# Block attention with a gated MLP: from heads with split operands to pairs of heads in plain float32

## The chip, the cores and the metric

The kernel runs on one core of one Trainium2 chip. The metric is the device time in microseconds. Two runs of the kernel before took 1095.97 and 1096.88 us, median 1096.43 us.

## The reference

Attention over 8 batches of 8 heads, 576 positions, head size 64, with a mask by blocks of 64 positions. A gated MLP follows, and all of it is in float32:

```python
scores = (1/sqrt(64)) * q @ k.T              # per batch and head: 576 x 576
scores = where(i // 64 >= j // 64, scores, -1e9)
attn = exp(scores - max(scores)); attn = attn / (sum(attn) + 1e-9)
x = attn @ v                                 # heads side by side: 576 x 512 per batch
h = gelu_tanh(x @ w_in)                      # 576 x 1024
u, v = h[:, :512], h[:, 512:]
v_n = (v - mean(v)) / sqrt(var(v) + 1e-6) * g_ln
v_s = w_sg @ v_n + b_sg                      # mixes the 576 positions
out = x + (u * v_s) @ w_out
```

q and k come transposed (64 x 576 per head), v as 576 x 512 per batch; w_in, w_sg and w_out arrive in float64 or float32 and are split once into a high and a low part.

## The kernel before

Five engines work from queues of their own: PE (matrix products and transposes into PSUM banks of 512 columns), DVE and ACT (elementwise, both read PSUM), POOL (elementwise in SBUF), and SP, which issues every DMA. Each queue is worked off in order. The order within each queue is set by a scheduler when the program is built, from the order of the code and estimated times, so the code says what depends on what, and the built program what stands behind what.

**Products in two precisions.** `F32R` operands go through PE in one pass per column. To keep the precision, a float32 operand is cast to F32R (the high part) and the rest is kept as a second F32R operand (the low part). Plain `F32` operands need no split.

**Scores** (`load_qk`, `split_qk`, `Scores`, line 419). A head has only 64 rows of q and k. `load_qk` loads each head's q and k twice, into both halves of the 128 partitions (line 156). `split_qk` makes `q_s` (upper half the high part of q, lower half its rest: cast on DVE at line 94, subtraction on POOL at line 221), `k_h` (cast on ACT, line 94) and `k_l` (subtraction on POOL, line 222). One product with all 128 rows then gives high and low of q at once, and two products, with k_h and k_l, give the scores. The raw tiles `q_f` and `k_f` have one buffer each. The 576 query positions are cut into five row tiles i = 0 to 4 of 64, 128, 128, 128 and 128 rows, and tile i needs only its first 64, 192, 320, 448 or 576 key columns: 1600 columns per head, in four banks.

**Softmax.** `maximum` (DVE, line 432) masks, scales and takes the row maximum of a bank into the tile `prob`, `exponent` (ACT, line 446) exponentiates in place and sums.

**Values** (`Values`). `turn0`, `turn2` and `turn1` transpose `prob` on PE into a bank `ptj` (line 472), `high` casts it to `pt_h` (ACT, line 483), `low` makes `pt_l` (DVE, line 491), and `av0`, `av2`, `av1` multiply (line 538). `v_s` holds the high and the low part of v side by side in 128 columns, and so the result `ob` has the two parts in its two halves, which `fold` adds (a copy on ACT, an addition on DVE). `inverse`, `turn_sums` and `rows` spread the reciprocal row sums over a tile `rb`, and `normalise` multiplies on POOL, spills the result x to DRAM for the residual, and splits it for the MLP. The transposed banks come from a pool `p` of three, all others from a pool `s` of five.

`FAP` and `FSP` make exceptions for early pairs of heads: the first eight pairs (batches 0 and 1) take their products with the values in plain float32 ("w", line 518), pairs 0 and 3 their scores too, and pair 1 splits its scores in three products ("p").

**The MLP** is cut in pieces: `v_part` (5 pieces, accv, line 718), `u_part` (8, accu, line 794), `s_part` (8, accs, line 834), `o_part` (8, acco, line 858). `slot(n)` emits for head n the transposes and products with the values, and for head n + 1 the scores; at four places it takes pieces of the previous batch's MLP from the queue `work` (`PLAN`: how many at each place). At the end of a batch `begin` appends `v`, the `o` of the batch before, `u` and `s`. During the first batch there are no pieces yet; weights are loaded and split instead (`WS`: steps per head). After the last batch the rest of the MLP runs alone.

Of the kernel before, what the change touches and what calls it, by code (L numbers as in the profile page):

```python
# [11 lines left out]
I32 = mybir.dt.int32  # L12
# [15 lines left out]
def kernel(  # L28
# [28 lines left out]
    KINDS = dict(x.split(":") for x in 'x:x3,xr:r2,xh:y4,xl:z4,vv:a9,vh:a9,vl:a9,u:b10,gh:b10,gl:b10,q_d:a9,w:a9'.split(","))  # L57
    AB = 'a'
    Q0 = 'v'
    OB0 = int('0')  # L60
    TB = int('2')
    OTB = int('1')
    CH = int('1')
    KB = int('2')
    QB = int('1')
    WF = int('2')
    RE = 'p'
    XB = int('10')

    cp = ctx.enter_context(tc.tile_pool(name="cp", bufs=1))  # L70
    ld = ctx.enter_context(tc.tile_pool(name="ld", bufs=1))
# [3 lines left out]
    BK = dict(x.split(":") for x in 's:s5,o:s5,p:p3,a:s5'.split(","))  # L75

    def bank(use, name):
        tag = BK[use]
        return psum.tile([P, 512], F32, tag=tag[0], name=name, bufs=int(tag[1]))

    def page(dtype, n, name):
        kind = KINDS.get(name, KINDS["w"])
        return sp.tile([P, n], dtype, tag=kind[0], name=name, bufs=int(kind[1:]))


    loaded = {}
    qk_parts = {}
    v_parts = {}

    AC = 'k'  # L90
    WL = 'pppv'

    def cpy(c, dst, src):
        (nc.scalar.copy if c in AC else nc.vector.tensor_copy)(dst, src)  # L94

    P0 = int('1')
    A0 = int('8')
    F0 = 'va'
    A4 = int('0')
    VB = int('1')  # L100
    FAP = 'wwwwwwww'
    FSP = 'wpsw'

    def values_mode(b, h):

        n = (b * H + h) // 2
        return FAP[n] if n < len(FAP) else "s"

    def scores_mode(b, h):
        n = (b * H + h) // 2  # L110
        return FSP[n] if n < len(FSP) else "s"

    FE = 'vavv'
    LN = int('0')
    L0 = int('1')
    V0 = 'v'
    H1 = 'aa'
    H00 = 'vvgg'
    H0 = 'ga'

    DQ = ''

    def dma(c):
        return nc.scalar.dma_start if c in DQ else nc.sync.dma_start

    KO = int('2')
    KH = 'x'
    KL = 'x'
    KE = 'v'

    def eng(c):
        return {"v": nc.vector.tensor_copy, "a": nc.scalar.copy, "g": nc.gpsimd.tensor_copy}[c]

    def pin(b, h, ins, e="v"):
        return tc.keep_in_program_order(ins) if b * H + h < KO and e in KE else ins

    def load(b, h):
        if scores_mode(b, h) != "s":
            q_f = k_f = None
            if h % 2 == 0:  # L140
                if h // 2 % 2 < L0:
                    q_f = ld.tile([P, S], F32, tag="q_f", name="q_f")
                    k_f = ld.tile([P, S], F32, tag="k_f", name="k_f")
                else:
                    q_f, k_f = page(F32, S, "q_d"), page(F32, S, "q_d")
                dma("q")(q_f, qT[b, h : h + 2].rearrange("a d s -> (a d) s"))
                dma("q")(k_f, kT[b, h : h + 2].rearrange("a d s -> (a d) s"))
        else:
            q_f, k_f = load_qk(b, h)
        load_v(b, h, q_f, k_f)  # L150

    def load_qk(b, h):
        q_f = ld.tile([P, S], F32, tag="q_f", name="q_f")
        k_f = ld.tile([P, S], F32, tag="k_f", name="k_f")
        for dst, src in ((q_f, qT), (k_f, kT)):
            dma("q")(dst, src[b, h].unsqueeze(0).broadcast_to([2, D, S]))
        return q_f, k_f

    def load_v(b, h, q_f, k_f):
        v_f = None  # L160
        if h % 2 == 0:

            whole = values_mode(b, h) == "w"
            if whole:
                v_f = sp.tile([P, NT, 2 * D], F32, tag="v_s", name="v_f", bufs=2)
            else:
                v_f = ld.tile([P, NT + 1, 2 * D], F32, tag="v_f", name="v_f", bufs=VB)
            cols = slice(h * D, (h + 2) * D)
            dma("v")(
                v_f[:, : NT - 1, :],  # L170
                v[b, : (NT - 1) * P, cols].rearrange("(j p) d -> p j d", p=P),
            )
            if whole:
                dma("v")(v_f[:TAIL, NT - 1, :], v[b, S - TAIL :, cols])
            else:
                ends = v[b, :, cols].rearrange("(j p) d -> p j d", p=BLK)[:, :: S // BLK - 1, :]
                for hf in (0, 1):
                    dma("v")(v_f[hf * BLK : (hf + 1) * BLK, NT - 1 :, :], ends)
        loaded[b, h] = (q_f, k_f, v_f)

    def split_qk(b, h):
        q_f, k_f, _ = loaded[b, h]
        if scores_mode(b, h) != "s":


            if q_f is None:
                return
            if scores_mode(b, h) == "w":
                for hf in (0, 1):
                    r = slice(hf * D, (hf + 1) * D)  # L190
                    qk_parts[b, h + hf] = [(q_f[r, :], k_f[r, :])]
                return
            if h % 4 == 0:
                q_h = sp.tile([P, S], F32R, tag="q_s", name="q_h", bufs=QB)
                k_h = sp.tile([P, S], F32R, tag="k_h", name="k_h", bufs=QB)
                k_l = sp.tile([P, S], F32R, tag="k_l", name="k_l", bufs=QB)
                q_l = page(F32R, S, "q_d")
            else:
                q_h, k_h, k_l, q_l = (page(F32R, S, "q_d") for _ in range(4))
            e = H00 if h == 0 else H0 + "gg"  # L200
            sub = {"v": nc.vector.tensor_tensor, "g": nc.gpsimd.tensor_tensor}
            pin(b, h, eng(e[0])(q_h, q_f), e[0])
            pin(b, h, eng(e[1])(k_h, k_f), e[1])
            pin(b, h, sub[e[2]](k_l, k_f, k_h.bitcast(F32), op=ALU.subtract), e[2])
            pin(b, h, sub[e[3]](q_l, q_f, q_h.bitcast(F32), op=ALU.subtract), e[3])
            for hf in (0, 1):
                r = slice(hf * D, (hf + 1) * D)
                qk_parts[b, h + hf] = [
                    (x[r, :], y[r, :]) for x, y in ((q_h, k_h), (q_l, k_h), (q_h, k_l))
                ]  # L210
            return
        q_s = sp.tile([P, S], F32R, tag="q_s", name="q_s", bufs=QB)
        k_h = sp.tile([P, S], F32R, tag="k_h", name="k_h", bufs=QB)
        k_l = sp.tile([P, S], F32R, tag="k_l", name="k_l", bufs=QB)
        if b == 1:
            eng(H1[0])(q_s, q_f)
            eng(H1[1])(k_h, k_f)
        else:
            cpy("q", q_s, q_f)
            cpy("k", k_h, k_f)  # L220
        nc.gpsimd.tensor_tensor(q_s[D:, :], q_f[D:, :], q_s[D:, :].bitcast(F32), op=ALU.subtract)  # L221
        nc.gpsimd.tensor_tensor(k_l, k_f, k_h.bitcast(F32), op=ALU.subtract)  # L222
        qk_parts[b, h] = [(q_s, k_h), (q_s, k_l)]

    def split_v(b, h):
        v_f = loaded[b, h][2]
        if v_f is None:
            return
        if values_mode(b, h) == "w":
            v_parts[b, h] = v_parts[b, h + 1] = v_f  # L230
            return
        v_s = sp.tile([P, NT + 1, 2, 2, D], F32R, tag="v_s", name="v_s", bufs=2)
        src = v_f.rearrange("p j (a d) -> p j a d", a=2)
        hi = v_s[:, :, :, 0, :]
        lo = v_s[:, :, :, 1, :]
        if b == 0:
            pin(b, h, eng(V0)(hi, src), V0)
        else:
            nc.scalar.copy(hi, src)
        pin(b, h, nc.gpsimd.tensor_tensor(lo, src, hi.bitcast(F32), op=ALU.subtract), "g")  # L240
        v_parts[b, h] = v_parts[b, h + 1] = v_s

    load(0, 0)


    ident = cp.tile([P, P], F32, name="ident")
    make_identity(nc, ident)
    W0 = int('18')
    if W0:

        t = bank("a", "warm")
        for _ in range(W0):
            nc.tensor.transpose(t[:, :P], ident, ident)

    MW = EXT[NT - 2]
    MB = int('1')
    mask = cp.tile([P, MW], mybir.dt.bfloat16 if MB else F32, name="mask")
# [5 lines left out]
    nc.gpsimd.memset(stats, 1.0)  # L263
    prob = []
    for s in (0, 1):
# [715 lines left out]
    if N > 1:  # L981
        load(*heads[1])
# [78 lines left out]
```

## Time and profile before

| | |
|---|---|
| median of the runs | 1096.43 us |
| profiled execution | 1098.28 us |
| its span, first to last instruction | 1096.5 us |
| mean granted clock of PE | 0.897 |
| busy: PE, DVE, ACT, POOL | 941.7, 634.7, 539.5, 524.4 us |
| matrix instructions | 5470 |
| moved by DMA | 85.16 MB, mean 78 GB/s |

Lines of the profile name an engine, a line of the code, an operation and its tiles (out<-in). In a timeline the first column is the start in us, the second the duration, xN the number of instructions merged in the row, and the bracket at the end the idle time of the engine before it and what ended it. In the table by windows each engine's busy time stands with its number of instructions in brackets, then the clock granted to PE as a share of full speed, the share of the 16 DMA engines that was busy, and GB/s. In the list of waits stand the total in us, the number of waits, and the longest. In the groups of instructions stand busy us and mean ns of one, then the idle time before them and what ended most of it. A matrix instruction's recorded end is modelled: instructions of a pipeline overlap in the rows, so a price per column is taken from starts, or from many instructions in a stretch without gaps.

### The profile page before, as it was taken

How to read it: one execution, taken by the hardware profiler on the slowest of the kernel's cores; microseconds unless marked ns; L12 is line 12 of the kernel's file. 1: busy time of each engine (PE TensorE's matmuls, PEld its weight loads, DVE VectorE, ACT ScalarE, POOL GpSimd, SP SyncE). 2: the span in 40 equal slices, each digit the busy share in tenths (PEclk: the TensorE clock that was granted, in tenths of full speed). 3: DMA queues.
4: the chain of work that ended last, by engine and by line, in shares of the span. 5: the costliest groups of instructions: out<-in, count | busy, mean ns of one | idle time of the engine just before them, and what ended most of it. 6: DMA issues, size and time to landing. Idle time of an engine off the chain costs nothing.

```text
span 1096.5 us, 16116 instructions
## 1 busy us (share of the span) xinstructions
PE 941.7 (86%) x5470; PEld 773.4 (71%) x5470; DVE 634.7 (58%) x1828; ACT 539.5 (49%) x1351; POOL 524.4 (48%) x528
## 2 busy tenths in 40 slices
PE   9998798969789797895978979699686987779998
PEld 5554465747678686794867867697576976679898
DVE  3476345657666565674565746576365764467343
ACT  3454376346546473563726536464364734446240
POOL 2343356734357443674337733485334843257342
PEclk7598899989889998898988989799897998979999
DMA  4322121232212123211231122211222112211021
GB/s 151 101 96 79 66 87 56 88 101 84 105 66 75 44 97 99 76 69 49 75 113 62 66 75 99 75 65 55 82 86 76 66 60 78 100 66 45 22 88 65
DMA packets 58638, 85.16 MB, mean 78 GB/s; under 512 B 3770, under 2 KB 26810, under 8 KB 58556
## 3 DMA queue, kind: packets, MB, share of 16 engines
q1 hardware_dynamic: 58556, 84.14, 22.8%
q8 instruction: 43, 0.70, 0.3%
q14 instruction: 39, 0.32, 0.1%
HBM read 65.25 MB, written 18.87 MB: 77 GB/s over the span
## 4 chain that ended last, share of the span: by engine, by line
DMA 42%; PE 36%; ACT 9%; POOL 5%; DVE 5%; issue 3%; SPq 1%; POOLq 0%; ACTq 0%; DVEq 0%
DMA q_f<-in_qT 16%; DMA out_T<-xr 12%; DMA k_f<-in_kT 12%; PE accv L718 7%; PE ptj L472 6%; PE accu L794 5%; PE accs L834 5%; ACT prob L446 4%; PE s L419 4%; PE ob L518 3%; PE ob L538 3%; POOL q_s L221 3%; PE acco L858 2%; POOL k_l L222 2%; DMA xr<-spill 1%
## 5 line engine op out<-in xcount | busy, mean ns | idle before, releaser
L472 PE MATMUL ptj<-ident,prob 128*128 128x128 f32 (+1 forms) x896 | 171.7, 296 | 71.6 <-DVE pt_l L491 42.2
L222 POOL TENSOR_TENSOR k_l<-k_f,k_h 128x576 fp32r<-128x576 f32 x58 | 85.3, 1471 | 247.9 <-ACT k_h L94 213.4
L446 ACT ACTIVATE prob<-prob,negm 128x576 f32<-128x576 f32 (+4 forms) x320 | 177.4, 556 | 51.6 <-DVE negm L432 50.2
L472 PEld LDWEIGHTS ptj<-ident,prob 128*128 128x128 f32 (+1 forms) x896 | 110.3, 147 | 127.3 <-issue 76.7
L432 DVE CUSTOM_DVE_ANT_0 prob<-s,mask 128x448 f32<-128x448 f32 (+4 forms) x320 | 124.3, 422 | 33.3 <-PE s L419 32.1
L491 DVE TENSOR_TENSOR pt_l<-ptj,pt_h 128x512 fp32r<-128x512 f32 x144 | 94.2, 661 | 75.4 <-ACT pt_h L483 72.7
L221 POOL TENSOR_TENSOR q_s<-q_f,q_s 64x576 fp32r<-64x576 f32 x58 | 85.5, 1475 | 97.8 <-DVE q_s L94 61.6
L483 ACT CAST pt_h<-ptj 128x512 fp32r<-128x512 f32 x144 | 82.8, 582 | 71.4 <-PE ptj L472 53.2
L538 PE MATMUL ob<-pt_h,v_s 128*128 128x512 f32 (+4 forms) x240 | 80.9, 339 | 40.6 <-ACT pt_h L483 40.6
L419 PE MATMUL s<-k_h,q_s 128*128 128x288 f32 x348 | 105.3, 326 | 3.1 <-DVE xr L866 3.0
L94 ACT CAST k_h<-k_f 128x576 fp32r<-128x576 f32 x50 | 33.6, 671 | 147.2 <-DMA k_f<-in_kT 141.9
L94 DVE CAST q_s<-q_f 128x576 fp32r<-128x576 f32 x50 | 27.6, 552 | 122.3 <-DMA q_f<-in_qT 122.3
L419 PE MATMUL s<-k_l,q_s 128*128 128x288 f32 x348 | 91.1, 302 | 0.0
L794 PE MATMUL accu<-xh,wi_h 128*128 128x288 f32 x256 | 82.8, 323 | 0.0
L858 PE MATMUL acco<-gh,wo_h 128*128 128x288 f32 x256 | 81.4, 319 | 0.0
L794 PE MATMUL accu<-xh,wi_l 128*128 128x288 f32 x256 | 80.6, 315 | 0.0
L794 PE MATMUL accu<-xl,wi_h 128*128 128x288 f32 x256 | 80.3, 314 | 0.0
L538 PEld LDWEIGHTS ob<-pt_h,v_s 128*128 128x128 f32 x240 | 46.5, 194 | 47.4 <-ACT pt_h L483 42.7
L858 PE MATMUL acco<-gl,wo_h 128*128 128x288 f32 x256 | 79.7, 311 | 0.0
L858 PE MATMUL acco<-gh,wo_l 128*128 128x288 f32 x256 | 79.4, 310 | 0.0
L834 PE MATMUL accs<-ws_h,vh 128*128 128x288 f32 x256 | 77.5, 311 | 0.1
L834 PE MATMUL accs<-ws_h,vl 128*128 128x288 f32 x256 | 76.7, 302 | 0.0
(130 smaller groups left out, 2496.2 us busy)
## 6 DMA issues: line engine op xcount, KB each, us to landing
q_f<-in_qT SPq DMA_DIRECT2D x59, 288.0 KB
k_f<-in_kT SPq DMA_DIRECT2D x59, 288.0 KB
spill<-x SPq DMA_DIRECT2D x32, 288.0 KB
xr<-spill SPq DMA_DIRECT2D x32, 288.0 KB
out_T<-xr SPq DMA_DIRECT2D x32, 288.0 KB
v_f<-in_v SPq DMA_DIRECT2D x32, 256.0 KB
wraw<-in_w_in SPq DMA_DIRECT2D x16, 256.0 KB
v_f<-in_v SPq DMA_DIRECT2D x48, 64.0 KB
```

The costliest lines, as they stand in the source:

```text
L221: nc.gpsimd.tensor_tensor(q_s[D:, :], q_f[D:, :], q_s[D:, :].bitcast(F32), op=ALU.subtract)
L222: nc.gpsimd.tensor_tensor(k_l, k_f, k_h.bitcast(F32), op=ALU.subtract)
L419: nc.tensor.matmul(t[rows, off : off + hi - lo], qq[:, QS[i] : QS[i] + n], kk[:, lo:hi], start=(p == 0), stop=(p == len(self.terms) - 1),)
L432: pin(self.b, self.h, nc.vector.tensor_tensor_reduce(self.pr[i][r, lo:hi], self.where[i, lo][r, :], mask[r, MW - (hi - lo) :] if 0 < i and ...
L446: pin(self.b, self.h, nc.scalar.activation(self.pr[i][r, :e], self.pr[i][r, :e], AF.Exp, bias=self.negm[r, i : i + 1], scale=-1.0, accum_o ...
L472: nc.tensor.transpose(dst, self.pr[i][r0 : QN[i], P * j : P * (j + 1)], ident[r0 : QN[i], r0 : QN[i]],)
L483: pin(self.b, self.h, nc.scalar.copy(hi[:, :n], t[:, :n]), KH)
L491: pin(self.b, self.h, nc.vector.tensor_tensor(lo[:, :m], t[:, :m], hi[:, :m].bitcast(F32), op=ALU.subtract), KL)
L538: nc.tensor.matmul(dst, w, t[:, c0 : c0 + n], start=start and x == 0, stop=stop and x == len(terms) - 1)
L794: nc.tensor.matmul(acc[:, :SH], w[:, c, fs], a[:, ts], start=(c == 0 and y == 0), stop=(c == NC - 1 and y == 2),)
L834: nc.tensor.matmul(acc[:, :SH], l, r, start=(y == 0), stop=(y == len(terms) - 1))
L858: nc.tensor.matmul(acc[:, :SH], w[:, c, ms], a[:, ts], start=(c == 0 and y == 0), stop=(c == NC - 1 and y == 2),)
```

## The change

The unit of attention becomes the pair of heads. q and k of two heads are loaded once, one head in the upper and one in the lower 64 partitions, into two buffers each, two pairs ahead. The scores of the two heads are plain float32 products in PE's two row halves, each into a bank of its own, written one after the other in the code. A transposed bank is copied once (`out`; four of a pair's six copies on ACT, two on DVE) into a float32 tile `pt`. The products with the values of the two heads are plain float32 products that fill the two column halves (partitions 0 to 63 and 64 to 127 of one bank `ob`). `normalise` multiplies on DVE straight from the banks. The casts, subtractions and `fold` are gone, and with them the exceptions for early pairs. `PLAN` has five places per pair, `begin` appends `v`, `u`, the `o` of the batch before, `s`, and the weights are loaded in the slots of the first eight pairs. All matrix products are now issued from line 85, all transposes from line 88.

```diff
-    def load_qk(b, h):
-        q_f = ld.tile([P, S], F32, tag="q_f", name="q_f")
-        k_f = ld.tile([P, S], F32, tag="k_f", name="k_f")
-        for dst, src in ((q_f, qT), (k_f, kT)):
-            dma("q")(dst, src[b, h].unsqueeze(0).broadcast_to([2, D, S]))
-        return q_f, k_f
+    def load_qk(n):
+        b, h = PAIRS[n]
+        q_f = sp.tile([P, S], F32, tag="q_f", name="q_f", bufs=2)
+        k_f = sp.tile([P, S], F32, tag="k_f", name="k_f", bufs=2)
+        nc.sync.dma_start(q_f, qT[b, h : h + 2].rearrange("a d s -> (a d) s"))
+        nc.sync.dma_start(k_f, kT[b, h : h + 2].rearrange("a d s -> (a d) s"))
+        qk[n] = (q_f, k_f)
...
         def products(self, *parts):
-            t = bank("s", "s")
+            t = [sbank("s"), sbank("s")]
             off = 0
             for i, lo, hi in parts:
-                self.where[i, lo] = t[:, off : off + hi - lo]
                 n, rows = QN[i], slice(0, QN[i])
-                for p, (qq, kk) in enumerate(self.terms):
-                    nc.tensor.matmul(
-                        t[rows, off : off + hi - lo],
-                        qq[:, QS[i] : QS[i] + n],
-                        kk[:, lo:hi],
-                        start=(p == 0),
-                        stop=(p == len(self.terms) - 1),
-                    )
+                for a in (0, 1):
+                    r = slice(a * D, (a + 1) * D)
+                    dst = t[a][rows, off : off + hi - lo]
+                    self.where[a, i, lo] = dst
+                    mm(dst, self.q[r, QS[i] : QS[i] + n], self.k[r, lo:hi], start=True, stop=True)
                 off += hi - lo
...
+    TE = {(0, 0): "a", (1, 0): "v", (0, 2): "a", (1, 2): "v", (0, 1): "a", (1, 1): "a"}
...
+        def out(self, a, j, t):
+            pt = self.pt[a, j] = sp.tile([P, 512], F32, tag="pt", name="pt", bufs=4)
+            copy(TE[a, j], pt, t)
...
+        def av(self, dst, j, pts, c0, n, start, stop):
+            for a in (0, 1):
+                r = slice(a * D, (a + 1) * D)
+                mm(dst[r, :], self.v[:, j, r], pts[a][:, c0 : c0 + n], start=start, stop=stop)
...
         def normalise(self):
-            x = xraw.pop((b, p))
-            nc.gpsimd.tensor_tensor(x, x, self.rb, op=ALU.mult)
+            x = self.x = page(F32, S, "x")
+            nc.vector.tensor_tensor(x[:, :BLK], self.o0, self.rb[:, :BLK], op=ALU.mult)
+            nc.vector.tensor_tensor(x[:, BLK:], self.ob, self.rb[:, BLK:], op=ALU.mult)
...
-    WS = [int(x) for x in '1 2 1 1 2 0 4 3 5 0 2 2 4 2 1 2 0 1 1 1 3 1 4 3 0 0'.split()]
+    WS = [2, 5, 7, 8, 3, 2, 1, 1]
...
-    PLAN1 = '1111 1120 1011 1010 0111 1011 1000 2111'.split()
-    PLAN = '1111 1120 1101 2101 1111 1120 2111 1111'.split()
+    PLAN = ["12211", "12211", "12211", "12222"]
...
+    def slot(n, sc):
+        va = Values(n, sc)
+        nx = Scores(n + 1) if n + 1 < N else None
+        g = [int(x) for x in PLAN[n % 4]]
+        if n + 2 < N:
+            load_qk(n + 2)
+        if n + 1 < N:
+            load_v(n + 1)
+        va.inverse()
+        if nx:
+            nx.step1()
+        va.turn0(0)
+        va.turn0(1)
+        if nx:
+            nx.step2()
+        hole(g[0])
+        load_share(n, 0)
+        run_side(4)
+        va.av0()
+        va.turn2(0)
+        va.turn2(1)
+        if nx:
+            nx.step3()
...
-                    work.extend([v_] + before + [u_, s_])
+                work.extend([v_, u_, *last_o, s_])
```

Where the scheduler puts this is seen in the built programs. On PE, in a steady batch, the scores of one head stood before as pairs of passes into one bank (`k_h` and `k_l` are the two parts of k, `s_` with its number the bank):

```order
L419 MATMUL s_6223<-k_h_6130,q_s_6129 128x288
L419 MATMUL s_6223<-k_l_6131,q_s_6129 128x288
L419 MATMUL s_6223<-k_h_6130,q_s_6129 128x192
L419 MATMUL s_6223<-k_l_6131,q_s_6129 128x192
L419 MATMUL s_6234<-k_h_6130,q_s_6129 128x448
L419 MATMUL s_6234<-k_l_6131,q_s_6129 128x448
```

Now the two heads of a pair take turns where the products of a step stand as the code writes them (the banks 4357 and 4358 belong to the first and the second head):

```order
L85 MATMUL s_4357<-k_f_4118,q_f_4117 128x288
L85 MATMUL s_4358<-k_f_4118,q_f_4117 128x288
L85 MATMUL s_4357<-k_f_4118,q_f_4117 128x192
L85 MATMUL s_4358<-k_f_4118,q_f_4117 128x192
L88 MATMUL pa_4369<-ident_70,prob2_4_134 128x128
```

and elsewhere the scheduler puts one head's bank before the other's, with the small product of row tile 0 between the partners:

```order
L85 MATMUL s_4181<-k_f_3812,q_f_3811 128x448
L85 MATMUL s_4181<-k_f_3812,q_f_3811 64x64
L85 MATMUL s_4182<-k_f_3812,q_f_3811 128x448
L85 MATMUL s_4182<-k_f_3812,q_f_3811 64x64
L85 MATMUL ob_4162<-pt_4152,v_f0_101 64x512
```

Counted over the whole program, a score product stands directly ahead of its equal partner for 60% of the score columns.

The products with the values on PE, before, with the high and the low part of the transposed probabilities as operands:

```order
L538 MATMUL ob_6294<-pt_h_6256,v_s_5770 128x512
L538 MATMUL ob_6294<-pt_l_6267,v_s_5770 128x512
L572 MATMUL ptj4_6319<-ident_76,prob1_0_116 64x64
L632 MATMUL ptj4_6319<-ident_76,rx_6248 128x128
L538 MATMUL ob_6294<-pt_h_6264,v_s_5770 128x320
L538 MATMUL ob_6294<-pt_l_6269,v_s_5770 128x320
```

and now, with the tiles `pt` of the first and the second head as operands:

```order
L85 MATMUL ob_4162<-pt_4171,v_f0_101 64x320
L85 MATMUL ob_4162<-pt_4179,v_f0_101 64x320
L85 MATMUL ob_4162<-pt_4171,v_f0_101 64x192
L85 MATMUL ob_4162<-pt_4179,v_f0_101 64x192
L88 MATMUL pc_4233<-ident_70,prob0_1_110 128x64
```

Where high and low part followed each other, the two heads do; for 76% of these columns a product stands directly ahead of its partner.

On SP's queue the loads of a head stood before with a wait for POOL, whose subtraction is the last reader of the raw tile (the names DMAHW are the semaphores of earlier DMAs):

```order
L646 DMA spill<-x 128x576 [waits Pool_49]
L156 DMA k_f<-in_kT 128x1x576 [waits DMAHW4_49,Pool_49]
L156 DMA q_f<-in_qT 128x1x576 [waits DMAHW5_49,Pool_49]
L156 DMA q_f<-in_qT 128x1x576 [waits DMAHW3_49,Pool_49]
L156 DMA k_f<-in_kT 128x1x576 [waits DMAHW2_49,Pool_49]
```

and now with a wait for PE, whose products of two pairs earlier are the last reader of the buffer:

```order
L113 DMA v_f1_103<-in_v 128x4x128 [waits DMAHW4_49,PE_49]
L117 DMA v_f1_103<-in_v 64x128 [waits DMAHW5_49,PE_49]
L443 DMA spill_2957<-x_2954 128x576 [waits DVE_49]
L105 DMA q_f_3268<-in_qT 128x576 [waits PE_49]
L106 DMA k_f_3269<-in_kT 128x576 [waits DMAHW0_49]
```

There are half as many loads of q and k, they are no longer duplicated, and between two pairs' loads stand a pair's v and spill.

More of the change, by code (lines that the diff above doesn't have):

```diff
@@ L86 @@
[L86 to L111, printed above, removed]
@@ L181, in split_qk @@
[L181 to L223, printed above, removed]
@@ L225, in split_v @@
[L225 to L241, printed above, removed]
@@ new lines, in turn, with copy @@
+    def turn(out, in_, identity):
+        return pin(nc.tensor.transpose(out, in_, identity), "P")
+    def copy(e, dst, src):
+        f = {"v": nc.vector.tensor_copy, "a": nc.scalar.copy, "g": nc.gpsimd.tensor_copy}[e]
+        return f(dst, src)
+    PAIRS = [(b, h) for b in range(B) for h in range(0, H, 2)]
+    N = len(PAIRS)
+    qk = {}
+    vals = {}
+    v_bufs = []
+    def load_qk(n):
[5 more added lines that the diff above has]
+        qk[n] = (q_f, k_f)
@@ L246, with load_v @@
+    def load_v(n):
+        b, h = PAIRS[n]
+        v_f = v_bufs[n % 2]
+        cols = slice(h * D, (h + 2) * D)
+        nc.sync.dma_start(
+            v_f[:, : NT - 1, :],
+            v[b, : (NT - 1) * P, cols].rearrange("(j p) d -> p j d", p=P),
+        )
+        nc.sync.dma_start(v_f[:TAIL, NT - 1, :], v[b, S - TAIL :, cols])
+        vals[n] = v_f
+    load_qk(0)
     ident = cp.tile([P, P], F32, name="ident")
     make_identity(nc, ident)
[L248 to L253, printed above, removed]
+    t = sbank("warm")
@@ L255 @@
+    for _ in range(18):
+        nc.tensor.transpose(t[:, :P], ident, ident)
     MW = EXT[NT - 2]
-    MB = int('1')
-    mask = cp.tile([P, MW], mybir.dt.bfloat16 if MB else F32, name="mask")
+    mask = cp.tile([P, MW], BF16, name="mask")
     nc.gpsimd.memset(mask, 0.0)
@@ L263 @@
     nc.gpsimd.memset(stats, 1.0)
+    for s in (0, 1):
+        t = cp.tile([P, NT, 2 * D], F32, name=f"v_f{s}")
+        nc.gpsimd.memset(t[TAIL:, NT - 1, :], 0.0)
+        v_bufs.append(t)
+    pt0 = []
+    for s in (0, 1):
+        t = cp.tile([P, 2 * BLK], F32, name=f"pt0_{s}")
+        nc.gpsimd.memset(t[BLK:, :], 0.0)
+        pt0.append(t)
     prob = []
-    for s in (0, 1):
+    for s in range(4):
         row = []
@@ L961, in slot @@
-        load_share(n, 1)
-        run_side(SD[1])
-        if n + 3 < N:
-            load(*heads[n + 3])
-        fill(2)
+        hole(g[1])
+        run_gelu()
+        load_share(n, 1)
+        run_side(4)
+        va.av2()
+        va.turn1(0)
+        va.turn1(1)
+        va.turn_sums()
+        if nx:
+            nx.step4()
+        hole(g[2])
+        load_share(n, 2)
+        run_side(4)
         va.av1()
-        va.fold(busy)
-        load_share(n, 2)
-        run_side(SD[2])
-        fill(3)
+        va.normalise()
@@ L971, in slot @@
+        hole(g[3])
+        run_gelu()
         load_share(n, 3)
-        run_side(SD[3])
-        if h % 2 == 1:
-            pending.append(va.normalise)
+        run_side(4)
+        hole(g[4])
+        pending.append(va.split)
+        return nx
     pending = []
     last_o = []
-    SEQ = 'A'
-    split_qk(0, 0)
-    split_v(0, 0)
-    if N > 1:
-        load(*heads[1])
-    sc = Scores(0, 0)
-    for parts in (((4, 0, SH), (1, 0, EXT[1])), ((4, SH, S),), ((3, 0, EXT[3]), (0, 0, EXT[0])), ((2, 0, EXT[2]),)):
-        sc.products(*parts)
-        for part in parts:
-            sc.maximum(*part)
-            if part[2] == EXT[part[0]]:
-                sc.exponent(part[0])
@@ L990, with begin @@
[L990 to L994 removed]
+    load_v(0)
+    load_qk(1)
+    sc = Scores(0)
+    sc.step1()
+    sc.step2()
+    sc.step3()
+    sc.step4()
     for n in range(N):
[L996 to L1000 removed]
+        sc = slot(n, sc)
+        if n % (H // 2) == H // 2 - 1:
+            def begin(b=PAIRS[n][0]):
                 v_, u_, s_, o_ = feed_forward(b)
[L1002 to L1010 removed]
+                work.extend([v_, u_, *last_o, s_])
+                last_o[:] = [o_]
```

575 lines of the change are left out of this document (166 added, 409 removed).

## The prediction

> **What bounds the kernel now.** I read the granted clock first, then the busy time by stage, then who ended the waits, and last one such wait in order of time.
>
> ```profile
> core 0: 1096.5 us, clock 0.897
> PE 941.7 (86%) x5470; PEld 773.4 (71%) x5470; DVE 634.7 (58%) x1828; ACT 539.5 (49%) x1351; POOL 524.4 (48%) x528
> ...
> 0.00:200.00 200.00, 178.52 (x778) 110.52 (x779) 99.23 (x329) 100.37 (x264) 87.81 (x114) 0.84 0.28 91
> 200.00:1000.00 800.00, 670.34 (x4049) 574.85 (x4049) 490.02 (x1391) 412.22 (x1033) 399.44 (x375) 0.90 0.23 77
> 1000.00:1096.50 96.50, 92.81 (x647) 88.05 (x645) 45.42 (x110) 26.88 (x56) 37.14 (x41) 0.99 0.16 53
> ```
>
> The matrix engine (PE) is the only engine near its limit, but it is not at it. A mean clock of 0.897 over 1096.5 us loses 0.103 x 1096.5 = 113 us, and PE waits 1096.5 - 941.7 = 155 us. What is left, 1096.5 - 113 - 155 = 829 us, is PE's work at full clock. Of the two losses most lies in the steady stretch from 200 to 1000 us: 800 - 670.3 = 130 us of waits, and 0.10 x 800 = 80 us of clock. The last 96 us (feed-forward alone) lose almost nothing, and the change leaves their work alone.
>
> The waits of PE in four whole batches (433.5 to 966 us), with the sum of the windows of that stretch, and after them two rows of the list for all engines over the whole span:
>
> ```profile
> sum 532.50, PE 444.58 PEld 385.72 DVE 321.07 ACT 273.72 POOL 265.26; mean PE 111.14 PEld 96.43 DVE 80.27 ACT 68.43 POOL 66.31
> PE ob L538 <- ACT pt_h L483: 34.4, 4, 9.6
> PE ptj L472 <- DVE pt_l L491: 28.3, 4, 7.8
> PE ptj L472 <- ACT rb L637: 14.9, 4, 3.9
> ...
> ACT k_h L94 <- DMA k_f<-in_kT: 141.9, 20, 10.3
> DVE q_s L94 <- DMA q_f<-in_qT: 122.3, 35, 8.8
> ```
>
> PE waits 532.5 - 444.6 = 88 us there, and 34.4 + 28.3 + 14.9 = 77.6 us of it (88%) are twelve long waits, three in each batch, for ACT or DVE. Those two in turn wait for q and k to land, because the casts k_h and q_s stand in their queues ahead of everything else. One of the twelve, from issue to release:
>
> ```profile
> 498.09 0.51 SPq L156 DMA_DIRECT2D k_f<-in_kT  x1
> 510.82 0.67 ACT L94 CAST k_h<-k_f 128x576 fp32r<-128x576 f32 x1 [10.09 <-DMA k_f<-in_kT]
> 511.52 0.58 ACT L483 CAST pt_h<-ptj 128x512 fp32r<-128x512 f32 x1
> 512.16 0.79 PE L538 MATMUL ob<-pt_h,v_s 128*128 128x512 f32 x1 [9.46 <-ACT pt_h L483]
> ...
> 498.10:510.30 12.20, 4.60 (x28) 3.49 (x27) 3.42 (x14) 1.83 (x5) 0.73 (x1) 0.77 0.13 48
> 504.80:515.00 10.20, 2.84 (x7) 2.26 (x8) 2.75 (x5) 4.13 (x10) 3.17 (x3) 0.50 0.09 31
> 1.00:6.00 5.00, 4.20 (x19) 3.87 (x20) 0.00 (x0) 1.01 (x1) 1.60 (x16) 1.00 0.85 264
> ```
>
> The load of k_f is issued at 498.09, when its one buffer is free again, and its cast starts at 510.82: 12.7 us for 288 KB, with 0.13 of the DMA engines busy. At the start of the kernel, where the first pair's q, k and v are loaded without the duplication onto two halves, the share is 0.85 and the rate 264 GB/s. So the duplicating load is slow as well as late. After the wait the clock is 0.50 for some 10 us: the wait is paid once as idle time and again as slow work. The bound of the steady stretch is this ring (load, cast, subtraction on POOL, buffer free, next load).
>
> **The change part by part.** *1. The loads.* q and k are loaded once per pair, in the form of the early loads, into two buffers each, and nothing casts them; PE reads them directly. In the order of SP (in the section on the change) a load waited for POOL before and waits now for PE's products of two pairs earlier, which are done about a pair ahead of need. SP's queue still holds spill, xr and out_T ahead of some loads; a pair now takes some 28 us, against the few us that one such entry waits. I take all twelve of these waits as gone: 88% of the 130 us, **-114 us**. The clock loss follows them (80 us x 0.88): **-70 us**. If the loads were late anyway, both terms would be nought.
>
> *2. The products.* Prices per column, all at full clock: the f32r form in the last feed-forward stretch and in one product with the values, and plain float32, of which the first pairs of this kernel already have some.
>
> ```profile
> 1066.00:1079.00 13.00, 13.00 (x100) 13.00 (x99) 1.00 0.00 0
> 434.54 0.39 PE L538 MATMUL ob<-pt_h,v_s 128*128 128x512 f32 x1
> 434.77 0.40 PE L538 MATMUL ob<-pt_l,v_s 128*128 128x512 f32 x1
> 435.00 0.31 PE L538 MATMUL ob<-pt_h,v_s 128*128 128x320 f32 x1
> ...
> 5.83 5.36 PE L419 MATMUL s<-k_f,q_f 64*128 64x288 f32 x22
> 77.45 1.07 PE L518 MATMUL ob<-pt_h,v_f 128*64 128x512 f32 x2 [0.45 <-DVE pt_h L481]
> 78.46 0.24 PE L572 MATMUL ptj<-ident,prob 64*64 64x64 f32 x1
> ```
>
> 100 f32r passes of 288 columns take 13.00 us, 0.451 ns a column; the two passes of 512 columns at 434.54 take 0.46 us, the same. A float32 product is two rows of the trace: the 22 rows at 5.83 are eleven products with 1600 + 1280 = 2880 columns in 5.36 us, 1.86 ns a column, and the product of 512 columns at 77.45 takes 1.01 us until the next row, 1.97 ns a column. So float32 costs four passes where the split costs two, and pays only if two products run at once.
>
> They do in the row halves, in the one place of this trace where the end of one head's scores (rows 0 to 63) meets the start of the next head's (rows 64 to 127). The timeline cut to 8.69-8.70 us, then to 9.00-9.05 us, gives:
>
> ```profile
> 8.62 0.53 PE L419 MATMUL s<-k_f,q_f 64*128 64x320 f32 x2
> 8.62 0.80 PE L419 MATMUL s<-k_f,q_f 64*128 64x320 f32 x4
> ```
>
> Two instructions are in flight at 8.70, and all four of a 320-column and a 288-column product are done in 0.80 us; at 1.86 ns their 608 columns alone are 1.13 us. Here the Trainium skill differs ("TensorE: Matmul & The Clock Gate", Part 3, The mechanism): matmuls start strictly in program order, so the second head could begin only with the first product's second instruction, which cannot have started by 8.70. The trace decides for me. For column halves no row of this trace has two neighbours. I bound them by full overlap and by none, and take overlap, by the nearest row, that of the row halves. The same page (Part 3, Measured speedup vs the span model) gives 2.38 times for three column tiles of 32. At that efficiency, an estimate, the sum would be some 20 us more.
>
> In the new order a product stands directly ahead of its partner for 60% of the score columns and 76% of the columns of the products with the values (counted over all rows); those I take at half price.
> - Scores, before: 58 heads x 3200 columns x 0.451 = 84 us, and 16 us for the early pairs (four heads in plain float32, two in three passes): 100 us. After: 64 x 1600 x 1.86 = 190 us alone, x (1 - 0.30) = 133 us. **+33 us**.
> - Values, before: 48 heads x 3072 x 0.451 = 66 us and 16 heads x 1600 x 1.97 = 50 us: 117 us. After: 64 x 1600 x 1.97 = 202 us alone, x (1 - 0.38) = 125 us. **+8 us**.
>
> Together +41 us; -21 us if every column overlapped, +118 us if the column halves did not, +175 us if neither did. Transposes and feed-forward keep their counts.
>
> *3. The other engines.* The casts, subtractions and folds go. The largest groups:
>
> ```profile
> L491 DVE TENSOR_TENSOR pt_l<-ptj,pt_h 128x512 fp32r<-128x512 f32 x144 | 94.2, 661 | 75.4 <-ACT pt_h L483 72.7
> L483 ACT CAST pt_h<-ptj 128x512 fp32r<-128x512 f32 x144 | 82.8, 582 | 71.4 <-PE ptj L472 53.2
> L221 POOL TENSOR_TENSOR q_s<-q_f,q_s 64x576 fp32r<-64x576 f32 x58 | 85.5, 1475 | 97.8 <-DVE q_s L94 61.6
> L222 POOL TENSOR_TENSOR k_l<-k_f,k_h 128x576 fp32r<-128x576 f32 x58 | 85.3, 1471 | 247.9 <-ACT k_h L94 213.4
> L446 ACT ACTIVATE prob<-prob,negm 128x576 f32<-128x576 f32 (+4 forms) x320 | 177.4, 556 | 51.6 <-DVE negm L432 50.2
> ```
>
> In their place six copies of 512 columns per pair remain (four on ACT, 128 x 0.58 = 74 us; two on DVE). All three engines end below 60% of a 950 us span, so these savings are worth nothing directly; PE covers them. Their worth is a shorter chain from transpose to product.
>
> *4. The first batch.* The first 105 us have no feed-forward to fill with:
>
> ```profile
> 0.00:105.00 105.00, 96.72 (x365) 55.39 (x366) 53.17 (x185) 48.21 (x141) 36.55 (x62) 0.76 0.32 103
> 13.40:54.00 40.60, 40.60 (x122) 22.88 (x123) 17.02 (x63) 15.93 (x50) 9.89 (x14) 0.50 0.27 87
> ```
>
> Here the products are float32 already and PE is busy at half clock. Pairing halves part of them, but 22 of the 29 weight steps now fall here, 14 before. Between 0 and -30 us I take **-15 us**.
>
> *5. New waits.* The order now waits for ACT copies that stand behind exponentials and gelu. Before, only 10 of the 88 us of waits in four batches were of such kinds. I take that for seven batches and half of it away, **+10 us**.
>
> Sum: 1096.5 + 41 - 114 - 70 - 15 + 10 = 948.5 us of span. The profiled execution took 1098.28 us, 1.8 us more than its span, and the median of the runs is 1096.43 us, so the span stands for the median: **950 us**.
>
> **The rivals.**
> - *The column halves do not overlap* (row halves do): +118 in place of +41 us, 1027 us. For it: no row shows them. Against it: the row halves do.
> - *Neither overlaps, the change does not do what it says*: +175, 1084 us. Against it: the rows at 8.62.
> - *Products start in program order* (the rule above): an overlapped pair then takes three of four parts, scores 190 x 0.85 = 161 and values 202 x 0.81 = 164 us, +108 in place of +41: 1017 us. Against it: the row of two in flight.
> - *Copies take the place of the loads*: PE waits once in each of the 28 later pairs for a copy behind exponentials and gelu on ACT, as the 3.9 us waits for rb show, at 4 us with the clock that follows: +112, 1060 us. For it: four of six copies per pair sit on ACT with ten exponentials. Against it: feed-forward stands between many transposes and their product.
> - *Slower: the clock stays halved in attention.* From 13.4 to 54 us PE is 100% busy and still at 0.50, with just this mix of float32 products and transposes. The new order has stretches of a pair with no feed-forward. A transpose takes 0.11 us of PE:
>
> ```profile
> 442.78 0.60 PE L631 MATMUL rbp<-ident,rx 128*128 128x128 f32 x4
> 443.22 0.27 PE L632 MATMUL ptj<-ident,rx 128*128 128x128 f32 x1
> ```
>
> so the 1120 transposes are 123 us, and attention is (133 + 125 + 123) / 8 = 48 us of PE a batch; all of it at half clock in seven batches would add 336 us, 1286 us. It decides from 24 us a batch on: 7 x 24 = 168 us makes 1118 us. Against it: from 200 us on the clock is 0.90 with such stretches.
>
> **How the numbers follow.** Forecast 0.57 (900 to 1000 us), columns apart 0.13, neither 0.04, program order 0.05, copies 0.14, slower 0.07. The range 885 to 1050 us reaches from full overlap to columns apart with some new waits, and leaves out two in ten. A measurement of this kernel tells about 2% from no change (1074 to 1118 us): faster 0.85, same 0.08, slower 0.07.
>
> **What would show it.** Right: a clock of 0.95 or more from 200 us on; no long waits of ACT or DVE for q or k; a pair of 512-column products with the values in some 1.1 us, of 288-column scores in 0.6; first feed-forward near 90 us; PE busy over 90%. Wrong: partners one after the other (2.0 us for the 512 pair), or waits of over 3 us of PE for ACT's pt or rb in most pairs, or a clock near 0.8.

## The result and the profile after

The changed kernel takes 1051.07 us (median of 1049.36 and 1052.77), the kernel before 1096.43 us: a ratio of 0.9586, 95% interval 0.9517 to 0.9655. It is 45 us faster where 146 us were forecast, and just above the range. The profiled execution took 1052.77 us, with a span of 1050.8 us and a mean clock of 0.920. A run over 1.5% above the fastest of its kernel counts as slow, and times and ratios here are of the other runs (this leaves out two of the four runs of one control).

Two lines of its page, the engines' busy time and the clock granted to PE in 40 slices of the span:

```profile
PE 964.7 (92%) x5554; PEld 690.3 (66%) x5554; DVE 465.9 (44%) x1442; ACT 427.0 (41%) x1122; POOL 267.4 (25%) x341
...
PEclk7799999998989989899878999889989899869999
```

The loads are gone as a cause: q and k land in 2.9 and 3.2 us, and no wait in PE's list is for them. But the clock still dips about once a batch (130 us, 5 slices). The list of PE's waits says behind whom it stands now (total us, times, longest):

```profile
PE s L85 <- DVE negm L297: 23.7, 25, 4.1
PE acco L85 <- DVE xr L635: 10.9, 20, 1.6
PE acco L85 <- DVE negm L297: 8.5, 10, 1.4
PE ob L85 <- ACT pt L92: 6.6, 5, 5.4
```

A matrix product that waits for DVE's `negm` or `xr` waits for no operand of its own: those instructions empty banks. PE is short of banks, then, though the pool `s` has five. By windows, first the steady part, then a stretch of the third batch's period in which `o` runs:

```profile
200.00:1000.00 800.00, 741.45 (x4246) 540.26 (x4246) 328.77 (x1006) 306.05 (x787) 181.45 (x209) 0.91 0.16 52
377.00:390.00 13.00, 9.10 (x52) 5.80 (x51) 12.20 (x32) 3.75 (x11) 7.87 (x8) 0.86 0.09 26
390.00:435.00 45.00, 38.65 (x184) 26.70 (x185) 15.37 (x45) 12.79 (x36) 10.09 (x11) 0.81 0.18 59
```

In 58 us PE stands for 10.2 and runs at half clock for part of the rest; on both sides of it (333 to 377 and 435 to 456 us) it is busy throughout at 1.00. What holds the banks shows in ACT's timeline, cut to the copies that empty `accu` into `u` (line 578):

```profile
364.13 0.38 ACT L578 COPY u<-accu 128x288 f32<-128x288 f32 x1
364.86 0.40 ACT L578 COPY u<-accu 128x288 f32<-128x288 f32 x1 [0.35 <-PE accu L85]
432.36 1.31 ACT L578 COPY u<-accu 128x288 f32<-128x288 f32 x4
```

Four of a batch's eight accu sums are copied out late, all together at 432.4 us, though PE had finished the last of them at 376.6. They wait for pages. `u`, `gh` and `gl` of a batch take 4 + 4 + 4 tiles from one pool of 10 (`KINDS`, line 66). `begin` now runs `u` ahead of the `o` of the batch before, and until that `o` is done with `gh` and `gl` (8 pages), only two tiles of `u` have a page. The other two tiles' four sums stay in four of the five `s` banks. That leaves one bank for every other product into an `s` bank from 376.6 us until the copies at 432.4 us. This follows from the code and the times of the copies; the trace does not number the banks. PE's timeline shows what it is like:

```profile
421.24 0.29 PE L85 MATMUL acco<-gh,wo_l 128*128 128x288 f32 x1
422.08 1.07 PE L85 MATMUL s<-k_f,q_f 64*128 64x288 f32 x4 [0.55 <-DVE xr L635]
423.99 0.85 PE L85 MATMUL s<-k_f,q_f 64*128 64x288 f32 x1 [0.84 <-DVE negm L297]
```

PE sums an acco, waits for DVE to add it, does one head's scores (x4: the two instructions of a 288 and of a 192 column product), waits for their maximum, and only then starts the other head's. So it waits after each piece, its clock falls, and the two heads cannot run side by side.

### The profile page after: what moved, and what is told of

Read it like the earlier page. It is cut to its first block, busy times and chain, and to the rows that moved or that the text cites. A ratio compares the mean times of both kernels' runs of the same rounds, so it can differ in the third digit from the quotient of the medians.

```text
span 1050.8 us, 15018 instructions
## 1 busy us (share of the span) xinstructions
PE 964.7 (92%) x5554; PEld 690.3 (66%) x5554; DVE 465.9 (44%) x1442; ACT 427.0 (41%) x1122; POOL 267.4 (25%) x341
## 4 chain that ended last, share of the span: by engine, by line
PE 76%; DVE 13%; ACT 3%; DMA 2%; POOL 2%; issue 2%; SPq 1%; DVEq 0%; POOLq 0%; ACTq 0%
PE s L85 12%; PE accs L85 12%; PE acco L85 11%; PE ob L85 11%; PE accv L85 10%; PE accu L85 9%; PE pc L88 3%; PE pb L88 3%; DVE prob L297 3%; PE pa L88 2%; DVE bs L518 2%; DVE xr L635 2%; ACT prob L310 1%; PE pe L88 1%; DMA w<-in_w_in 1%
## 5 line engine op out<-in xcount | busy, mean ns | idle before, releaser
L310 ACT ACTIVATE prob<-prob,negm 128x448 f32<-128x448 f32 (+3 forms) x320 | 177.8, 556 | 235.5 <-DVE negm L297 234.1
L85 PE MATMUL s<-k_f,q_f 64*128 64x288 f32 (+4 forms) x768 | 193.9, 447 | 34.2 <-DVE negm L297 23.7
L297 DVE CUSTOM_DVE_ANT_0 prob<-s,mask 128x288 f32<-128x288 f32 (+2 forms) x320 | 122.2, 424 | 168.9 <-PE s L85 168.8
L85 PEld LDWEIGHTS s<-k_f,q_f 64*128 64x128 f32 (+1 forms) x768 | 88.9, 188 | 102.1 <-issue 40.3
L85 PE MATMUL ob<-pt,v_f 128*64 128x448 f32 (+4 forms) x640 | 129.5, 454 | 11.0 <-ACT pt L92 6.6
L611 POOL TENSOR_TENSOR gl<-u,gh 128x288 fp32r<-128x288 f32 x64 | 51.6, 807 | 154.6 <-DVE gh L610 151.9
L85 PEld LDWEIGHTS acco<-gh,wo_h 128*128 128x128 f32 x256 | 58.9, 230 | 31.8 <-DVE xr L635 16.6
L85 PE MATMUL accs<-ws_l,vh 128*128 128x288 f32 x256 | 75.1, 294 | 0.0
L85 PE MATMUL accv<-wi_h,xh 128*128 128x512 f32 x160 | 66.0, 413 | 0.0
L85 PE MATMUL accv<-wi_l,xh 128*128 128x512 f32 x160 | 63.4, 396 | 0.0
```

Of the source, the lines that this page charges most:

```text
L85: return pin(nc.tensor.matmul(*a, **k), "P")
L297: nc.vector.tensor_tensor_reduce(self.prob[a][i][r, lo:hi], self.where[a, i, lo], mask[r, MW - (hi - lo) :] if 0 < i and hi == e else mask ...
L310: nc.scalar.activation(self.prob[a][i][r, :e], self.prob[a][i][r, :e], AF.Exp, bias=self.negm[a][r, i : i + 1], scale=-1.0, accum_out=self ...
L611: nc.gpsimd.tensor_tensor(glo[:, ts], x, ghi[:, ts].bitcast(F32), op=ALU.subtract)
```

## The experiments

All ratios are to the kernel before, timed on the same chip in the same rounds.

**The old order of the parts in the changed kernel.**

```diff
-                work.extend([v_, u_, *last_o, s_])
+                work.extend([v_, *last_o, u_, s_])
```

> The changed kernel with the feed-forward's parts back in the order v, o of the batch before, u, s. Theory 'pages': in the changed kernel the third and fourth tile of u (10 pages, of which gh and gl of the batch before hold 8) get no page until the last products of acco are done, so four finished accu sums stand in four of the five s banks for some 55 us a batch (no copy of accu between 364.9 and 432.4 us), PE waits for the one bank that is left, and the clock falls. The stretch from 377 to 435 us loses 10.3 us to waits and 10.4 us to the clock; seven such batches are 145 us. Expected: 945 us, 920 to 985, clock from 200 to 1000 us above 0.96, waits of PE under 40 us in all. Rival 'VectorE burst': the layer norm's 15 us burst on DVE (375 to 391 us) delays the maxima, whatever the order: within 20 us of 1051. Rival 'the clock falls by itself' in stretches of float32 products and transposes: waits go, the clock stays near 0.92, some 1010 us.

908.69 us, ratio 0.8266 (0.8232 to 0.8300): 142 us less than the changed kernel, and below what I expected. The steady part by windows:

```profile
200.00:850.00 650.00, 650.00 (x4171) 477.72 (x4170) 299.06 (x990) 306.44 (x782) 172.75 (x205) 1.00 0.20 63
```

For 650 us PE never waits and never loses its clock, attention included. "The clock falls by itself" is out for this stretch, and DVE's burst, still there, costs PE no time in it.

**The new order in the kernel before**, which has a switch for it.

```diff
-    SEQ = 'A'
+    SEQ = 'B'
```

> The kernel before with one edit, its own switch for the order of the parts set to v, u, o, s as the changed kernel has it. Theory 'pages': it has the same ten pages and the same five banks, so four of them stand full for as long and it loses 10 to 20 us in each of seven batches: 1165 to 1235 us. Rival 'VectorE burst' or 'clock by itself': the order costs nothing by itself, within 20 us of 1096.

1241.99 us, ratio 1.1301 (1.1270 to 1.1331), 143 us more. The same sign in ACT's copies, and PE's two longest waits:

```profile
427.75 0.38 ACT L802 COPY u<-accu 128x288 f32<-128x288 f32 x1
508.24 1.31 ACT L802 COPY u<-accu 128x288 f32<-128x288 f32 x4
```

```profile
PE acco L858 <- DVE xr L866: 53.2, 18, 8.8
PE ob L538 <- ACT pt_h L483: 40.5, 5, 8.2
```

The second four come 80 us after the first here. The order costs 142 us in the changed kernel and 143 us in the kernel before, with pairs as with heads.

**More pages, in the changed kernel's own order.** This takes the pages apart from whatever else the order does: 12, 11 and, as a control, 10 pages, with two small pools cut for the room in all three.

```diff
-    KINDS = {"x": ("x", 3), ...
-    KINDS.update({n: ("b", 10) for n in ("u", "gh", "gl", "w")})
+    KINDS = {"x": ("x", 2), ...
+    KINDS.update({n: ("b", 12) for n in ("u", "gh", "gl", "w")})   # 11; 10
...
-    for s in (0, 1):
+    for s in (0,):            # pt0: one tile, not two
```

> The changed kernel in its own order v, u, o, s, with 12 pages in place of 10 for u, gh, gl and the weights, so that all of u has a page while gh and gl of the batch before are still held. Room for them comes from x (2 tiles, not 3) and pt0 (1, not 2). Theory 'pages': no accu sum waits in its bank, and the 142 us between the changed kernel and the one in the old order go for the most part: 915 us, 895 to 950. Rival 'order': what costs is that o's additions (DVE, one for each acco sum) now fall into the layer norm's time on DVE, whatever the pages: 1000 us or more.

> As the one with 12 pages, but with 11. Theory 'pages': u's third tile gets a page and its fourth doesn't, so two of the five s banks stand full and not four; three stay in use, and most of the loss goes: 950 us, 915 to 1000, between the two others. Rival 'order': within 20 us of 1051.

> The control of the two: 10 pages as in the changed kernel, with x at 2 tiles and pt0 at 1. Both theories: within 15 us of 1051. If it is far below, x or pt0 matter, and the other two say less about pages; if far above, the smaller pools cost, and the gain by pages is larger than it looks.

12 pages: 906.70 us, ratio 0.8267 (0.8221 to 0.8313). 11 pages: 914.74 us, 0.8323 (0.8293 to 0.8352). Control: 1041.12 and 1042.87 us, 0.9486 (0.9448 to 0.9523), for 0.9586 of the changed kernel, so the smaller pools cost nothing. So pages it is, and not the place of `o`: with 12 the new order is as fast as the old one. The end of the row of copies, with 12 pages and with 11:

```profile
353.09 0.40 ACT L578 COPY u<-accu 128x288 f32<-128x288 f32 x1 [2.57 <-PE accu L85]
354.64 0.40 ACT L578 COPY u<-accu 128x288 f32<-128x288 f32 x1 [1.14 <-PE accu L85]
```

```profile
348.24 0.40 ACT L578 COPY u<-accu 128x288 f32<-128x288 f32 x1 [0.61 <-PE accu L85]
388.85 0.70 ACT L578 COPY u<-accu 128x288 f32<-128x288 f32 x2
```

With 12 each copy follows its sum; with 11 the last two are held back to 388.9 us. I had expected 950 us of that one, some 40 us above the old order. It is 8 us above 12 pages, and the two intervals overlap: three banks are nearly as good as five, and one alone costs 142 us.

**DVE's burst**, the rival to pages: the layer norm's side steps handed out two at a time.

```diff
-        run_side(4)     # four places
+        run_side(2)
```

> The changed kernel with the layer norm's side steps handed out two at a time and not four, so that the burst on DVE is spread over twice the time; the order of the parts is unchanged. Theory 'pages': the banks are held as long as before, within 15 us of 1051. Rival 'VectorE burst': the waits for negm (23.7 + 8.5 us) and the clock that follows them go for the most part, 1000 us or less.

1036.45 us, ratio 0.9436 (0.9405 to 0.9467): 15 us of the 142, and the waits for negm hardly shrink (27.9 + 2.9 us, for 23.7 + 8.5). The burst is a small matter beside the banks. The same edit in the old order:

> The kernel in the old order with the layer norm's side steps two at a time. In the changed kernel this gave 15 us, beside the held banks. Theory: those 15 us were banks freed late by maxima behind the burst, and with all five banks in turn nothing is left of them: 909 us within 8. Rival: the burst has a cost of its own: some 895.

930.10 us, ratio 0.8507 (0.8473 to 0.8541): 26 us slower by the ratios than with four, which neither expectation had. PE's waits rise from 23.5 to 40.0 us. The second row below is new: PE waits for the layer norm itself, which is not done when `s` begins. The first stood in the old order with four at a time too (7.7 us, 2 waits):

```profile
PE s L85 <- DVE negm L297: 9.8, 2, 5.9
PE accs L85 <- DVE vh L541: 8.4, 6, 2.6
```

**The loads alone, in the kernel before.**

```diff
-            dma("q")(dst, src[b, h].unsqueeze(0).broadcast_to([2, D, S]))
+            for hf in (0, 1):
+                dma("q")(dst[hf * D : (hf + 1) * D, :], src[b, h])
```

> The kernel before with one edit: each duplicated load of q or k (12.2 us) becomes two loads of 64 partitions, with the same bytes. This is the prediction's first term by itself. If it was right (114 us of waits for these loads and 70 us of clock that follow them), 912 us, 890 to 960. If another wait comes in place of half of them, some 1000. If these waits cover others of the same length, within 20 us of 1096.

915.81 us, ratio 0.8331 (0.8307 to 0.8355): 183 us less, against the prediction's 184. Each load lands in 2.8 us, and the steady part reads:

```profile
200.00:850.00 650.00, 630.66 (x4076) 556.15 (x4077) 506.46 (x1376) 408.13 (x1021) 395.28 (x370) 0.98 0.30 90
```

The Trainium skill states why one transfer was so slow ("DMA: Bandwidth & Descriptors", Rules for kernel authors): an outermost dimension of c copies confines a whole DMA to at most c engines. The trace agrees: 12.2 us for the copy to two halves, with 0.13 of the 16 engines busy, which is two of them, and 2.8 us for each half by itself.

**The halves apart**, in the old order. For the values each head's v gets 64 columns of zeros beside it, for the scores each head's q 64 rows of zeros, and both take the whole array. For this the loads of v and of q are split by head, and the room comes from pt0 and x as above, which cost nothing in the control:

```diff
-                r = slice(a * D, (a + 1) * D)
-                mm(dst[r, :], self.v[:, j, r], pts[a][:, c0 : c0 + n], start=start, stop=stop)
+                w = self.v[:, j, a : a + 2, :].rearrange("p a d -> p (a d)")    # [v_a, 0, v_b]
+                mm(dst, w, pts[a][:, c0 : c0 + n], start=start and a == 0, stop=stop and a == 1)
```

```diff
-                    mm(dst, self.q[r, QS[i] : QS[i] + n], self.k[r, lo:hi], start=True, stop=True)
+                    mm(dst, self.q[a][:, QS[i] : QS[i] + n], self.k[:, lo:hi], start=True, stop=True)
```

> The kernel in the old order (908.7 us), with the products with the values no longer in column halves: each head's stationary is widened to 128 columns by a block of zeros (v as [v_a, 0, v_b]), so both heads' products take the whole array and add into the same bank, as many columns as before. This prices the prediction's second term. Overlapping column halves: 77 us by the prediction's 76% of overlapped columns, less up to 20 us for some 210 changes of tile shape that go: 940 to 985 us. If column halves did not overlap: 909 us or less.

> The kernel in the old order (908.7 us), with the scores no longer in row halves: q of each head lies in a tile of its own with zeros in the other head's 64 rows, so both heads' products take all 128 rows with the whole of k, as many columns as before (x at 2 tiles and pt0 at 1 for the room, which cost nothing in their control). This prices the other half of the prediction's second term. Overlapping row halves: 57 us by the prediction's 60% of overlapped columns, less up to 15 us for some 160 changes of tile shape that go: 950 to 970 us. If row halves did not overlap: 909 us or less.

Values apart: 946.66 us, ratio 0.8616 (0.8586 to 0.8647). Scores apart: 939.76 us, 0.8602 (0.8575 to 0.8630). By ratios, 38 and 37 us more than with halves. The groups of the products, of the old order first, then values apart, then scores apart (busy us, mean ns of one):

```profile
L85 PE MATMUL s<-k_f,q_f 64*128 64x288 f32 (+4 forms) x768 | 149.1, 431 | 7.8 <-DVE negm L297 7.7
L85 PE MATMUL ob<-pt,v_f 128*64 128x320 f32 (+4 forms) x640 | 147.0, 443 | 6.6 <-ACT pt L92 6.3 <-DVE negm L297 0.2
```

```profile
L85 PE MATMUL ob<-pt,v_f 128*128 128x512 f32 (+4 forms) x640 | 204.7, 449 | 6.7 <-ACT pt L92 6.3 <-issue 0.3
```

```profile
L85 PE MATMUL s<-k_f,q_f 128*128 128x288 f32 (+4 forms) x768 | 210.5, 404 | 3.6 <-DVE negm L302 3.6
```

With halves the mean of one instruction is about the same (443 ns for 449) or longer (431 for 404), and the busy sum is 58 and 61 us smaller, so instructions run side by side in both kinds of halves. The kernel gets less than these sums. About 210 and 160 changes of tile shape go when the halves are given up; in the changed kernel's trace one takes some 0.1 us (an estimate from starts: the transpose at 65.35 us starts 0.34 us after the last instruction of a pair of scores, the instructions of that pair 0.24 us after each other), so they can be 21 and 16 us of it. No run prices them by themselves. With the scores apart, waits and clock lose 12 us less as well.

**Partners kept together**: TensorE in the written order, first with the old order of the parts, then with the new one and 12 pages.

```diff
-    PIN = ""
+    PIN = "P"
```

> The kernel in the old order with TensorE's instructions kept in the order in which they are written (PIN set to P), so that a head's product always has its partner's next to it and some 90 changes of tile shape go. PE is 97% busy, so its work counts in full: by the prediction's prices the last columns to overlap save up to 50 us, and 860 us come out if no wait takes their place. Rival: in the written order PE stands behind each copy and maximum that a reordering steps over: 920 us or more.

> The changed kernel in its own order v, u, o, s with 12 pages (x at 2 tiles, pt0 at 1) and TensorE's instructions in the written order: the two edits that helped, without the old order. If the order of the parts costs nothing by itself once u has its pages, it comes out with the pinned kernel in the old order, 882 us within 10. If order and pinning work against each other (o's additions on DVE in the layer norm's time, which a pinned PE cannot step over), 900 us or more.

In the old order 882.45 us, ratio 0.8080 (0.8050 to 0.8109): the fastest of all. The values' group falls from 147.0 to 114.6 us, the scores' from 149.1 to 137.4:

```profile
L85 PE MATMUL s<-k_f,q_f 64*128 64x288 f32 (+4 forms) x768 | 137.4, 437 | 7.3 <-DVE negm L297 7.2
L85 PE MATMUL ob<-pt,v_f 128*64 128x512 f32 (+4 forms) x640 | 114.6, 450 | 5.4 <-ACT pt L92 2.9 <-DVE pt L92 2.5
```

The second head's 512-column product with the values starts over 0.4 us after its partner in 10 of the 32 pairs, without pinning in 31. Some of the gain is paid back in waits (39.0 us for 23.5), so 882 and not the 860 I hoped for. With the new order and 12 pages pinning gives 901.37 us, 0.8214 (0.8161 to 0.8266). Order and pinning do work against each other, but the waits that I named for it (acco for xr) are 3.8 us. PE's work is 12 us longer, 11 of it in the 512-column products with the values, where the second head's product is late in 22 of the 32 pairs. In both pinned kernels every late one starts 0.05 to 0.06 us after DVE has finished copying its operand `pt`. So DVE is late with that copy more often in the new order, and it counts as work and not as a wait, because the first head's product runs meanwhile. Whether o's additions are what delays DVE is open.

## Why the prediction was wrong

A span divides into PE's waits (span less busy), half of the time in which PE was busy at half clock, and the rest, its work at full clock. From the traces, in us:

| kernel | span | waits | lost to half clock | work |
|---|---|---|---|---|
| before | 1096.5 | 154.8 | 77 | 864 |
| before, two loads | 913.3 | 29.2 | 26 | 858 |
| before, order v u o s | 1240.5 | 232.5 | 140 | 868 |
| changed | 1050.8 | 86.0 | 71 | 893 |
| changed, old order | 904.0 | 23.5 | 12 | 868 |
| changed, old order, pinned | 882.9 | 39.0 | 20 | 823 |

The change is then three steps: 1096.5 - 183 (loads) - 9 (the rest of the pairs, 904.0 against 913.3) + 147 (the order of the parts) = 1051. The prediction had -184, +36 and nothing.

- **The step that failed is the last one, which it did not have.** It wrote that the feed-forward keeps its count, and took 10 us for new waits, all behind ACT's copies. The line that moves `o` behind `u` stood in the diff and was priced at nothing. Its 147 us are 62 of waits, 59 of clock and 25 of work (the scores, whose partners cannot lie side by side in one bank, cost 35 us more, the transposes 7 more and the values 17 less, divided as in the table below). It could have been seen in the code: 4 + 4 + 4 pages of one pool of 10, and a step moved from behind their release to ahead of it. The Trainium skill names the sign ("Perfetto Trace Analysis", Optimization Strategy): the same gap over and over on the engine that should be saturated can mean that there is no room in SBUF or PSUM for the next tile. Here it was both, SBUF pages first and PSUM banks through them.
- **Term 1, the loads**: right, 183 for 184 us, and so close by luck, since the split was off. It had 114 us of waits and 70 of clock, and the runs show 126 of waits, 51 of clock and 7 of work. All of (1 - clock) x span had gone to the clock, 113 us, but of the 226 us at half clock PE was busy in only 155. So 77 us is what PE lost, and its work was 864 and not 829 us.
- **Term 2, the products**: mis-sized. The work rises from 858 to 868 us, 11 and not 41. That both halves overlap was right: a rival without overlapping column halves is out. The share of full cost was right in the scores (149.1 of 210.5 us, 0.71, for 0.70) and too low in the values (147.0 of 204.7, 0.72, for 0.62). Where the 30 us lie shows when each moment of PE's work, at full clock, is given to the instruction that started last (us):

  | | before, two loads | changed, old order | forecast |
  |---|---|---|---|
  | scores | 118 | 128 | 100, then 133 |
  | values | 136 | 140 | 117, then 125 |
  | transposes | 160 | 148 | the same |
  | feed-forward and warm-up | 444 | 453 | the same |

  The old products had been priced 37 us too low, from passes in an unbroken row; the new ones 10 us too low. So the products cost 15 us more and not 41, and transposes and feed-forward together 4 less.
- **Term 4, the first batch**: the first product of accv starts at 98.4 us, before at 109.4; -11 for -15. But with the two loads alone it starts at 95.4, so those 11 us belong to the loads, and the pairs save nothing there.
- **Term 5**: in the old order there are no new waits. They fall by 6 us against the kernel before with its loads mended, and the clock's loss by 14. Terms 2, 4 and 5 together came to -9 for +36 us, so without the order of the parts the forecast would have been some 41 us too high.
- **The rivals**: "copies take the place of the loads" has about the right time (1060 us) by the wrong mechanism; PE's waits for ACT, of any kind, are 16 us in all. "Slower: the clock stays halved in attention" is refuted by 650 us at 1.00. Program order (1017 us) has no run of its own, but its price, three of four parts for a pair, does not fit pairs that take no longer than one product (last section).
- **What would show it**: long waits for q and k gone, PE over 90% busy, and a pair of 512-column products with the values in 1.01 us and of 288-column scores in 0.59, all as written; the first feed-forward near 90 us was not (98.4), nor the clock of 0.95 from 200 us on: it was 0.91, and that pointed to what had been missed.

As for the pairs themselves: with the same order and mended loads they are 0.8266 for 0.8331, under 1% faster. They pay through what they make possible, whole partners side by side (0.8080 when pinned), and they leave DVE and ACT about half idle. The kernel before was not run pinned, so how much of that gain needs the pairs is not shown.

## What to carry to other kernels

Before a step is moved in a queue of work, count the tiles of each pool that it allocates against those that the steps it is moved past still have to release: a full pool holds the copy, the copy holds its PSUM bank, and PE ends up with the one bank that is left. When a sum of terms is right in parts and the whole is not, undo the edits one at a time, in the old kernel too: one line cost 143 us there as here, and two lines of loading gave 183. Look for the releaser of a wait one step further back: waits for `negm` and `xr` looked like a busy DVE, and DVE was 34% busy there (15.4 of the 45 us from 390 us on).

## What the hardware showed

Two products in different halves cost about what one costs. In PE's timeline, a score product of 288 columns by itself, then a pair of them in the two row halves (x2 and x4, since a float32 product is two instructions):

```profile
385.71 0.75 PE L85 MATMUL s<-k_f,q_f 64*128 64x288 f32 x2 [0.54 <-DVE negm L297]
```

```profile
63.85 0.76 PE L85 MATMUL s<-k_f,q_f 64*128 64x288 f32 x4
```

And a product of 512 columns with the values by itself (in the old order), then a pair of them in the two column halves (in the changed kernel); from the start to the next instruction it is 1.01 us both times:

```profile
305.24 1.07 PE L85 MATMUL ob<-pt,v_f 128*64 128x512 f32 x2
306.25 0.33 PE L88 MATMUL pb<-ident,prob 128*128 128x128 f32 x1
```

```profile
125.16 1.08 PE L85 MATMUL ob<-pt,v_f 128*64 128x512 f32 x4
126.17 0.33 PE L88 MATMUL pb<-ident,prob 128*128 128x128 f32 x1
```

And in the steady part the clock went with the gaps, not with the kind of work: float32 products and transposes at 100% busy keep it at 1.00 (the 650 us above), while the stretch from 390 to 435 us, with waits of half a microsecond after each piece, runs at 0.81. That about doubles what such waits cost (62 us of waits, 59 us of clock). It is not the whole rule: from 13.4 to 54 us the kernel before has PE busy throughout at 0.50, and what holds the clock down there is not shown.
